# Weight loads of two MLP layers issued by GpSimd instead of SyncE

## The chip, the core and the metric

The kernel runs on one core of one Trainium2 chip. The metric is the device time of one execution in microseconds. SyncE (SP) only issues transfers here; TensorE (PE), VectorE (DVE) and ScalarE (ACT) compute; GpSimd (POOL) does nothing in the kernel before beyond four fills at the start.

## What is computed

```python
# attention on 4 batches x 8 heads x 576 positions x 64, then two dense layers on 2304 tokens
out_d = sm_attn(q_d, k_d, v_d)                 # q, k, v averaged over 4 neighbours
out_up = np.repeat(out_d, factor, axis=2)
mask = np.abs(pos[:, None] - pos[None, :]) < factor          # a band of 7 keys
out_local = softmax(where(mask, scale * q @ k.T, -1e9)) @ v
x = (out_up + out_local) as [2304, 512]
h = x @ w_in                                   # 512 -> 2048
x = (maximum(h, 0) + alpha * minimum(h, 0)) @ w_out          # 2048 -> 512
h = x @ w_in2
out = where(h > 0, h, exp(minimum(h, 0)) - 1) @ w_out2
```

The weights arrive as 64-bit floats, so one tile of 128 by 512 is 512 KB.

## The kernel before

Each of the two layers has 32 weight tiles, i0, o0, i1, o1 and so on to i15, o15 (`items`): tile i of a pair feeds the matmuls x @ w_in, tile o those of @ w_out, for one slice of 128 hidden units. A tile is loaded raw (`load_w`, L314: name rawi or rawo) and then converted (`th_conv`, L1192): ACT copies the high half (cp), DVE shifts and merges it in three instructions (cp, cw, cw), ACT rounds the result (wi or wo) and DVE forms the remainder (wi or wo). Matmuls with a tile need all of it. PE runs the attention of the batches between the matmuls of the layers.

A Python scheduler writes the order of every engine's instructions when the kernel is built. It keeps a clock per engine (`_Clock`) with assumed costs, transfers included (`dma`, L166), and steps small generators ("threads") by priority. So a change in the assumed cost of a transfer moves instructions on all engines. All transfers stand in one queue, issued by SP in the written order; an SP instruction that waits for a semaphore holds all behind it.

The first batch uses buffers of later weight tiles: q and k lie in those of i12 to o15, v in those of i8 to o9 (`load_v0`), the operands of the dense local attention, vd and dP, in those of i6 to o7 and i4 to o5. `th_ldw` (L1226) lets a tile's load start only when its buffer is free: for i4 to o5 and i6 to o7 that is after the matmuls dP,vd of one of the four head pairs (`pav`). From the fifth tile on it also waits until the tile four places earlier is converted (`cv`, PF = 4).

The band of the first batch's second half goes through DRAM to be laid out as rows of 7: ACT copies scores to ss (two buffers), SP writes them to scr, SP reads the diagonal as s, DVE and ACT form the softmax a, SP writes a into pscr (a DRAM area filled with zeros by two transfers beforehand), SP reads it as pp, PE transposes pp (`th_S0`, `th_soft0`, `th_p`). ACT and DVE take their instructions in order, so an ss, s or ppT that is late holds the conversions behind it. xsp is a spill of x, mask a constant.

Of the kernel before, what the change touches and what calls it, by code (L numbers as in the profile page):

```python
# [7 lines left out]
F32 = mybir.dt.float32  # L8
# [9 lines left out]
NP = H // 2  # L18
# [24 lines left out]
PB, FB, RB, PF, CS = 1000.0, 300.0, 300.0, 4, 6  # L43
# [14 lines left out]
class _Clock:  # L58
# [2 lines left out]
           ("DVE", "DVE"): 127.0, ("DVE", "PE"): 179.0, ("DVE", "SP"): 120.0, ("PE", "ACT"): 197.0,  # L61
           ("PE", "DVE"): 196.0, ("PE", "SP"): 189.0, ("DMA", "SP"): 900.0, ("DMA", "ACT"): 907.0,
           ("DMA", "DVE"): 907.0, ("DMA", "PE"): 1003.0, ("ACT", "ACT"): 140.0}
    MANY = {"ACT": 70.0, "DVE": 93.0, "SP": 50.0, "PE": 0.0}

    def __init__(self):
        self.cols = {}
        self.t = dict.fromkeys(("PE", "ACT", "DVE", "SP", "DMA"), 0.0)
        self.t["SP"] = 560.0
        self.hw = 0.0  # L70
        self.seen = {}
        self.share = 1.0
        self.uses, self.bar, self.slots, self.count = {}, {}, {}, {}
        self.cur = self.ctx()
# [41 lines left out]
    def deps(self, eng, outs, ins):  # L116
# [13 lines left out]
        for src, e in last.items():  # L130
            if e > self.seen.get((eng, src), 0.0):
                self.seen[eng, src] = e
                n += 1
                t = max(t, e + self.LAG.get((src, eng), 0.0))
        return t + (self.MANY[eng] if n > 1 else 0.0)

# [26 lines left out]
            n, want = n * k, want * k  # L163
        return n * (8 if ap.dtype == U64 else 4)

    def dma(self, out, in_):  # L166
        outs, ins = [self.span(out)], [self.span(in_)]
        n = int(out.shape[0]) * _free(out) * (8 if out.dtype == U64 else 4)
        piece = min(self.run(out), self.run(in_))
        cost = max(n / 360 * (2 if piece < 512 else 1), n / piece / 16 * 7)  # L170
        self.t["SP"] = max(self.t["SP"], self.deps("SP", outs, ins))
        self.hw = max(self.hw + 25, self.t["SP"]) + 450
        end = max(self.t["DMA"], self.hw + 650) + cost
        self.t["DMA"] = end
        self.note("DMA", outs, ins, end)
        c = self.cur
        c["t"] = max(c["t"], end + 900)
        c["on"] = "DMA"


def _free(ap):
    n = 1
    for d in ap.shape[1:]:
        n *= int(d)
    return n


class _Engine:
# [31 lines left out]
    def __getattr__(self, op):  # L220
        fn = getattr(self.eng, op)

        def call(*args, **kw):
            if op == "dma_start":
                self.clock.dma(kw["out"], kw["in_"])
            else:
                outs = [kw[k] for k in ("out", "accum_out") if k in kw] + list(args[:1])
                ins = [a for k, a in kw.items() if k not in ("out", "accum_out") and hasattr(a, "ap")]
                wait = 0.6 * int(kw["lhsT"].shape[1]) if op == "matmul" else 0.0
                self.clock.op(self.name, *self.cost(op, kw, args), outs, ins + list(args[1:]), wait)  # L230
            return fn(*args, **kw)  # L231
        return call
# [3 lines left out]
def fused_kernel(ctx: ExitStack, tc: tile.TileContext, qk, vt, vl, ql, kl, vb, w_in1, w_out1, alpha,  # L236
                 w_in2, w_out2, ident_d, mask_d, zero_d, vd, maskd_d, out):
    nc = tc.nc
    ck = _Clock()
    PE, ACT, DVE, SP = (_Engine(n, e, ck) for n, e in  # L240
                        (("PE", nc.tensor), ("ACT", nc.scalar), ("DVE", nc.vector), ("SP", nc.sync)))

    const = ctx.enter_context(tc.tile_pool(name="const", bufs=1))
    wp = ctx.enter_context(tc.tile_pool(name="w", bufs=1))
# [10 lines left out]
    maskb = const.tile([128, 5, QK], BF16, name="maskb")  # L255
    identb = const.tile([128, 128], BF16, name="identb")
    warm = const.tile([128, 4], BF16, name="warm")

    W = {}
    raw = {}  # L260
# [51 lines left out]
    wsrc = {(1, "i"): w_in1, (1, "o"): w_out1, (2, "i"): w_in2, (2, "o"): w_out2}  # L312

    def load_w(key):  # L314
        ly, nm, f = key
        if wide:
            raw[key] = wp.tile([128, 512], U64, tag=f"w{nm}{f}", name=f"raw{nm}{f}")
            SP.dma_start(out=raw[key], in_=wsrc[ly, nm][f])

    gs = {}  # L320
    cp = {}
# [19 lines left out]
    st = {}  # L341
# [408 lines left out]
    def finish(*key):  # L750
        done[key] = ck.cur["t"]
# [474 lines left out]
    def th_ldw(ly):  # L1226
        for k, it in enumerate(items):
            if ly == 2:
                yield "key", "fr", (2,) + it
            else:  # L1230
                if PT0 <= k < PP0:
                    yield "key", "pav", 0, k - PT0, 0
                elif PP0 <= k < V0:
                    yield "key", "pav", 0, k - PP0, 0
                elif V0 <= k < SH0:
                    yield "key", "sv", 0, k - V0
                elif k >= QK0:
                    yield "key", "dav", (k - QK0) // 2, (1,)
                    for u in range(2):
                        yield "key", "smm", 0, (k - QK0) // 2, u  # L1240
                if k >= PF:
                    yield "key", "cv", 1, k - PF
            yield ("DMA",)
            load_w((ly,) + it)
            finish("ld", (ly,) + it)
            ck.cur["t"] = now[0]
# [185 lines left out]
    with tc.manual_schedule():  # L1432
# [32 lines left out]
        spawn(th_soft0(0, 1), -10, 0)  # L1465
        spawn(th_vb(0, 1), UV, 0)
        spawn(th_ldw(1), 0)
        for k in range(2 * NF):
            spawn(th_conv(1, k), k / CS, early=ECONV)
# [29 lines left out]
        for s in range(NS1 + NS2):  # L1499
            slot[0] = s if s else -1  # L1500
            ly, g, f, first, last, i = seq[s]
# [3 lines left out]
            if s == T7:  # L1505
                assert all(t["p"] < -50 for t in threads), [t["w"] for t in threads]
                pA.__exit__(None, None, None)
                pC = tc.tile_pool(name="pC", bufs=1)
                cp["pool"] = pC.__enter__()
                tokens.update({"x2": [0.0], "x2s": [0.0, 0.0], "cp": [0.0] * 2, "cw": [0.0] * 2, "os": [0.0] * 4})  # L1510
                spawn(th_ldw(2), 0)
                for k in range(2 * NF):
                    spawn(th_conv(2, k), 2 + k / 100)
                for gg in range(NG2):
                    spawn(th_x2(gg), gg)
# [5 lines left out]
            key = (ly, "i", f)  # L1521
# [124 lines left out]
```

## Time and profile before

| what | value |
|---|---|
| device time, median of 3 runs | 969.86 us (968.71 to 970.83) |
| device time of the profiled execution | 970.52 us |
| its span | 968.7 us |
| PE busy | 938.5 us, 97% of the span |
| DVE busy | 599.5 us, 62% |
| ACT busy | 471.3 us, 49% |
| transfers moved | 86.17 MB, mean 89 GB/s |

The span runs from the first to the last instruction that the profile shows; 1.8 us of the device time lie around it. All sums below start from the profiled execution. PE is busy in nearly all of the span, but before about 110 us it also runs short matmuls of no use (tile warm), runs part of the time at half clock, and waits.

### The profile page before, as it was taken

How to read it: one execution, taken by the hardware profiler on the slowest of the kernel's cores; microseconds unless marked ns; L12 is line 12 of the kernel's file. 1: busy time of each engine (PE TensorE's matmuls, PEld its weight loads, DVE VectorE, ACT ScalarE, POOL GpSimd, SP SyncE). 2: the span in 40 equal slices, each digit the busy share in tenths (PEclk: the TensorE clock that was granted, in tenths of full speed). 3: DMA queues.
4: the chain of work that ended last, by engine and by line, in shares of the span. 5: the costliest groups of instructions: out<-in, count | busy, mean ns of one | idle time of the engine just before them, and what ended most of it. 6: DMA issues, size and time to landing. Idle time of an engine off the chain costs nothing.

```text
span 968.7 us, 16336 instructions
## 1 busy us (share of the span) xinstructions
PE 938.5 (97%) x6428; PEld 866.0 (89%) x6428; DVE 599.5 (62%) x1253; ACT 471.3 (49%) x1200; POOL 0.2 (0%) x4
## 2 busy tenths in 40 slices
PE   5978999899999999999999999999999999999998
PEld 3767889799999899999999999989999999998997
DVE  5778998645959789899638999732322322322222
ACT  5575678555432572332326677644443433433433
POOL 0000000000000000000000000000000000000000
PEclk9687999989999999999999999999999999999999
DMA  9277762534111523100207950003100100000000
GB/s 291 93 247 228 240 222 52 102 110 160 50 31 54 167 70 90 33 19 37 82 1 238 377 195 33 1 1 98 55 12 1 66 1 1 33 1 1 33 1 32
DMA packets 60933, 86.17 MB, mean 89 GB/s; under 512 B 29279, under 2 KB 40415, under 8 KB 60599
## 3 DMA queue, kind: packets, MB, share of 16 engines
q1 hardware_dynamic: 60857, 85.14, 28.0%
q8 instruction: 50, 0.82, 0.4%
q14 instruction: 26, 0.21, 0.1%
HBM read 69.93 MB, written 16.63 MB: 89 GB/s over the span
## 4 chain that ended last, share of the span: by engine, by line
PE 89%; DMA 6%; ACT 2%; DVE 2%; issue 1%; SPq 1%; ACTq 0%
PE bank L231 89%; DMA scr<-ss 2%; DMA s<-scr 1%; DMA qk<-in_qk_dram 1%; DMA pp<-pscr 1%; DMA pscr<-a 1%; SPq L231 1%; ACT dP L231 0%; DVE cw L231 0%; ACT ss L231 0%; ACT cp L231 0%; ACT P L231 0%; DVE s L231 0%; ACT n L231 0%; DVE cp L231 0%
## 5 line engine op out<-in xcount | busy, mean ns | idle before, releaser
L231 PE MATMUL bank<-xh,wi 128*128 128x288 f32 x1024 | 240.6, 304 | 3.6 <-DVE wi L231 2.8
L231 ACT ACTIVATE n<-bank 128x288 f32<-128x288 f32 (+1 forms) x224 | 99.4, 444 | 290.7 <-PE bank L231 290.5
L231 PE MATMUL bank<-gh,wo 128*128 128x288 f32 x1024 | 237.1, 302 | 1.2 <-ACT ys L231 1.2
L231 PE MATMUL bank<-x2h,wi 128*128 128x384 f32 x768 | 211.2, 337 | 0.0
L231 PEld LDWEIGHTS bank<-xh,wi 128*128 128x128 f32 x1024 | 176.4, 191 | 8.6 <-DVE wi L231 3.9
L231 PEld LDWEIGHTS bank<-gh,wo 128*128 128x128 f32 x1024 | 174.4, 190 | 6.3 <-issue 2.9
L231 PE MATMUL bank<-wo,gh 128*128 128x512 f32 x576 | 179.0, 392 | 0.0
L231 DVE SCALAR_TENSOR_TENSOR r<-n,bank 128x384 f32<-128x384 f32 x96 | 53.1, 554 | 195.0 <-ACT n L231 194.9
L231 ACT ACTIVATE gh<-r 128x288 fp32r<-128x288 f32 (+1 forms) x224 | 106.8, 477 | 100.2 <-DVE r L231 99.7
L231 PE MATMUL bank<-xl,wi 128*128 128x288 f32 x512 | 152.9, 299 | 0.0
L231 PE MATMUL bank<-gl,wo 128*128 128x288 f32 x512 | 151.8, 297 | 0.0
L231 DVE TENSOR_TENSOR gl<-r,gh 128x288 fp32r<-128x288 f32 (+1 forms) x224 | 111.4, 498 | 60.8 <-ACT gh L231 59.2
L231 PEld LDWEIGHTS bank<-x2h,wi 128*128 128x128 f32 x768 | 140.3, 188 | 3.9
L231 PE MATMUL bank<-x2l,wi 128*128 128x384 f32 x384 | 128.9, 336 | 0.0
L231 PEld LDWEIGHTS bank<-wo,gh 128*128 128x128 f32 x576 | 106.8, 188 | 18.2
L231 PE MATMUL bank<-wo,gl 128*128 128x512 f32 x288 | 113.8, 395 | 0.0
L231 DVE SCALAR_TENSOR_TENSOR r<-n,nal,bank 128x288 f32<-128x288 f32 x128 | 65.2, 509 | 53.1 <-ACT n L231 52.5
L231 PEld LDWEIGHTS bank<-xl,wi 128*128 128x128 f32 x512 | 98.0, 191 | 0.0
L231 PEld LDWEIGHTS bank<-gl,wo 128*128 128x128 f32 x512 | 97.3, 190 | 0.0
L231 PEld LDWEIGHTS bank<-x2l,wi 128*128 128x128 f32 x384 | 72.1, 188 | 3.8
L231 PEld LDWEIGHTS bank<-wo,gl 128*128 128x128 f32 x288 | 54.0, 187 | 11.5
L231 ACT ACTIVATE n<-n 128x384 f32<-128x384 f32 x96 | 50.4, 525 | 3.1
(101 smaller groups left out, 895.6 us busy)
## 6 DMA issues: line engine op xcount, KB each, us to landing
rawi<-in_w_in_dram SPq DMA_DIRECT2D x32, 512.0 KB
rawo<-in_w_out_dram SPq DMA_DIRECT2D x32, 512.0 KB
qk<-in_qk_dram SPq DMA_DIRECT2D x12, 582.0 KB
yT<-ys SPq DMA_DIRECT2D x32, 144.0 KB
out_dram<-os SPq DMA_DIRECT2D x18, 256.0 KB
vl<-in_vl_dram SPq DMA_DIRECT2D x4, 960.0 KB
vv<-in_vt_dram SPq DMA_DIRECT2D x12, 288.0 KB
kls<-in_kl_dram SPq DMA_DIRECT2D x12, 288.0 KB
```

Source lines behind the costliest of these rows:

```text
L231: return fn(*args, **kw)
```

## The change

The loads of raw weight tiles are issued by GpSimd, on its own queue. GpSimd's first instruction is a copy of one column of the last v tile of the first batch into a new tile, pace; it waits until that v has landed, and all weight loads stand behind it. The wait of a load for the conversion four tiles earlier is gone; the waits for free buffers stay. The scheduler's clock gets an engine GP, whose transfers cost that engine 1000 units each.

```diff
-    def dma(self, out, in_):
+    def dma(self, out, in_, eng="SP"):
...
-        self.t["SP"] = max(self.t["SP"], self.deps("SP", outs, ins))
-        self.hw = max(self.hw + 25, self.t["SP"]) + 450
-        end = max(self.t["DMA"], self.hw + 650) + cost
+        self.t[eng] = max(self.t[eng], self.deps(eng, outs, ins))
+        if eng == "SP":
+            self.hw = max(self.hw + 25, self.t["SP"]) + 450
+            end = max(self.t["DMA"], self.hw + 650) + cost
+        else:
+            self.t[eng] += 1000
+            end = max(self.t["DMA"], self.t[eng] + 650) + cost
...
+    pace = const.tile([128, 1], F32, name="pace")
...
-            SP.dma_start(out=raw[key], in_=wsrc[ly, nm][f])
+            GP.dma_start(out=raw[key], in_=wsrc[ly, nm][f])
...
-                if k >= PF:
-                    yield "key", "cv", 1, k - PF
+                if not k:
+                    yield "key", "ldv", NP - 1
+                    nc.gpsimd.tensor_copy(out=pace, in_=st["vv", 0, NP - 1][:, 0:1])
```

The order of instructions shows what moves. First SP, from the second write of scores to the read s of the first batch; before:

```order
L231 DMA scr0_1_94<-ss_584 72x624 [waits DMAHW5_49,Activation_49]
L231 DMA rawo2_592<-in_w_out1_dram 128x512 [waits DMAHW6_49]
L231 DMA rawi3_623<-in_w_in1_dram 128x512 [waits DMAHW7_49]
L231 DMA rawo3_653<-in_w_out1_dram 128x512 [waits DMAHW0_49]
L231 DMA scr0_1_94<-ss_646 72x624 [waits DMAHW1_49,Activation_49]
L231 DMA vb_675<-in_vb_dram 78x2048 [waits DMAHW2_49]
L231 DMA rawi4_692<-in_w_in1_dram 128x512 [waits DMAHW3_49,PE_49]
L231 DMA scr0_1_94<-ss_671 72x624 [waits DMAHW4_49,Activation_49]
L231 DMA qk_724<-in_qk_dram 128x1164 [waits DMAHW5_49]
L231 DMA vv_726<-in_vt_dram 128x576 [waits DMAHW6_49]
L231 DMA rawo4_758<-in_w_out1_dram 128x512 [waits DMAHW7_49,PE_49]
L231 DMA s0_777<-scr0_1_94 72x32x7 [waits DMAHW4_49,DMAHW1_49,DMAHW0_49]
```

The same engine with the change, from the spill xsp on to the first pp:

```order
L235 DMA xsp_91<-x_375 128x1152 [waits DMAHW3_49,DVE_49]
L235 DMA mask_75<-in_mask_dram 128x182 [waits DMAHW4_49]
L235 DMA pscr1_99<-in_zero_dram 12x14982 [waits DMAHW5_49]
L235 DMA pscr0_98<-in_zero_dram 12x14982 [waits DMAHW6_49]
L235 DMA scr0_1_95<-ss_568 72x624 [waits DMAHW7_49,Activation_49]
L235 DMA scr0_1_95<-ss_600 72x624 [waits DMAHW0_49,Activation_49]
L235 DMA scr0_1_95<-ss_678 72x624 [waits DMAHW1_49,Activation_49]
L235 DMA scr0_1_95<-ss_716 72x624 [waits DMAHW2_49,Activation_49]
L235 DMA s0_762<-scr0_1_95 72x32x7 [waits DMAHW3_49,DMAHW2_49,DMAHW7_49,DMAHW1_49,DMAHW0_49]
L235 DMA pscr1_99<-a_845 72x32x7 [waits DMAHW5_49,DMAHW4_49,DVE_49]
L235 DMA pp_923<-pscr1_99 72x624 [waits DMAHW4_49]
L235 DMA pp_925<-pscr1_99 72x624 [waits DMAHW6_49]
```

All weight loads are gone from SP; vb, qk and vv, which stood between the writes of scr, come later, behind pp. GpSimd, which issued nothing, now begins like this (semaphores DMAHW belong to SP's transfers, DMASW to GpSimd's; pace and the first five loads):

```order
L1249 COPY pace_81<-v0_3_138 128x1 [waits DMAHW0_49]
L235 DMA rawi0_273<-in_w_in1_dram 128x512
L235 DMA rawo0_275<-in_w_out1_dram 128x512
L235 DMA rawi1_277<-in_w_in1_dram 128x512
L235 DMA rawo1_290<-in_w_out1_dram 128x512
L235 DMA rawi2_305<-in_w_in1_dram 128x512
```

and from the load of i5 on, whose buffer is that of the third dP, it goes on like this:

```order
L235 DMA rawi5_486<-in_w_in1_dram 128x512 [waits DVE_49,DMASW2_49,PE_49,Activation_49]
L235 DMA rawo5_535<-in_w_out1_dram 128x512 [waits DVE_49,DMASW3_49,PE_49,Activation_49]
L235 DMA rawi6_637<-in_w_in1_dram 128x512 [waits DMAHW1_49,DMASW4_49]
L235 DMA rawo6_654<-in_w_out1_dram 128x512 [waits DMAHW5_49,DMASW5_49]
L235 DMA rawi7_675<-in_w_in1_dram 128x512 [waits DMAHW1_49,DMASW6_49]
L235 DMA rawo7_686<-in_w_out1_dram 128x512 [waits DMAHW2_49,DMASW7_49]
L235 DMA rawi8_695<-in_w_in1_dram 128x512 [waits DMASW0_49]
L235 DMA rawo8_720<-in_w_out1_dram 128x512 [waits DMASW1_49,DVE_49]
L235 DMA rawi9_748<-in_w_in1_dram 128x512 [waits DMAHW4_49,DMASW2_49,DVE_49]
L235 DMA rawo9_788<-in_w_out1_dram 128x512 [waits DMASW3_49,DVE_49,Pool_49]
```

Up to o3 the loads wait for nothing but pace and GpSimd itself; i4 to o5 wait for PE, and i6 to o11 stand behind o5 with only waits for transfers and for work on v that is older, and each for the load eight places earlier.

Second, ACT around the third and fourth copy of scores (ss_646 and ss_671); before:

```order
L231 ACTIVATE P_603,dsum_627<-P_603,dmx_606 72x144 x2
L231 ACTIVATE n_630<-bank5_71 128x288
L231 ACTIVATE ss_646<-bank7_73 72x312
L231 ACTIVATE ss_646<-bank6_72 72x312
L231 ACTIVATE gh_636<-r_631 128x288
L231 ACTIVATE P_603<-P_603,dsum_627 72x144 x2
L231 ACTIVATE P_620,dsum_659<-P_620,dmx_650 72x144 x2
L231 ACTIVATE ss_671<-bank7_73 72x312
L231 ACTIVATE ss_671<-bank6_72 72x312
```

With the change (ss_678 and ss_716), from n on:

```order
L235 ACTIVATE n_644<-bank5_71 128x288
L235 ACTIVATE cp_649<-rawo2_326 128x512
L235 ACTIVATE P_617<-P_617,dsum_641 72x144 x2
L235 ACTIVATE gh_652<-r_645 128x288
L235 ACTIVATE P_634,dsum_663<-P_634,dmx_658 72x144 x2
L235 ACTIVATE ss_678<-bank7_73 72x312
L235 ACTIVATE ss_678<-bank6_72 72x312
L235 ACTIVATE wi2_683<-cw_627 128x512
L235 ACTIVATE P_634<-P_634,dsum_663 72x144 x2
L235 ACTIVATE cp_700<-rawi3_344 128x512
L235 ACTIVATE ss_716<-bank7_73 72x312
L235 ACTIVATE ss_716<-bank6_72 72x312
```

The third copy of scores now stands behind one more cp, the two P groups and gh; the fourth behind another wi and cp.

Third, DVE just ahead of the first softmax on s; before:

```order
L231 TENSOR_REDUCE dmx_785<-P_779 72x2
L231 TENSOR_SCALAR dmx_785<-dmx_785 72x2
L231 TENSOR_SCALAR cp_764<-cp_764 128x512
L231 TENSOR_TENSOR gl_776<-r_767,gh_775 128x288
L231 SCALAR_TENSOR_TENSOR wi3_795<-cw_740,wi3_795 128x512
L231 TENSOR_SCALAR dsum_799<-dsum_799 72x2
L231 RECIPROCAL dsum_799<-dsum_799 72x2
L231 SCALAR_TENSOR_TENSOR cw_817<-rawo3_653,cp_764 128x512
L231 SCALAR_TENSOR_TENSOR cw_817<-rawo3_653,cw_817 128x512
L231 SCALAR_TENSOR_TENSOR s2_820<-s0_777,mask_75 72x224
```

With the change:

```order
L235 SCALAR_TENSOR_TENSOR wi3_728<-cw_703,wi3_728 128x512
L235 SCALAR_TENSOR_TENSOR cw_750<-rawo3_363,cp_726 128x512
L235 SCALAR_TENSOR_TENSOR cw_750<-rawo3_363,cw_750 128x512
L235 SCALAR_TENSOR_TENSOR r_754<-n_753,nal_76,bank4_70 128x288
L235 TENSOR_SCALAR cp_735<-cp_735 128x512
L235 SCALAR_TENSOR_TENSOR cw_773<-rawi4_380,cp_735 128x512
L235 TENSOR_TENSOR gl_761<-r_754,gh_760 128x288
L235 SCALAR_TENSOR_TENSOR wo3_790<-cw_750,wo3_790 128x512
L235 SCALAR_TENSOR_TENSOR cw_773<-rawi4_380,cw_773 128x512
L235 SCALAR_TENSOR_TENSOR s2_807<-s0_762,mask_75 72x224
```

The softmax now stands behind the whole conversion of o3 and three steps of i4; a P block (dmx, dsum) that stood ahead of it comes later.

## Rows read from the trace of the kernel before

**Rows 1.** The page: the span, and PE's busy time with its share.

```profile
span 968.7 us, 16336 instructions
PE 938.5 (97%) x6428; PEld 866.0 (89%) x6428; DVE 599.5 (62%) x1253; ACT 471.3 (49%) x1200; POOL 0.2 (0%) x4
```

**Rows 2.** Windows: stretch, length, busy time of five engines, PE clock, DMA share, GB/s.

```profile
16.00:24.00 8.00, 6.37 (x60) 4.18 (x55) 7.54 (x23) 6.82 (x32) 0.00 (x0) 0.84 0.96 336
24.00:40.00 16.00, 16.00 (x148) 11.78 (x147) 11.64 (x30) 8.26 (x30) 0.00 (x0) 0.50 0.01 4
40.00:60.00 20.00, 16.96 (x161) 13.31 (x160) 14.95 (x34) 14.56 (x45) 0.00 (x0) 0.87 0.86 290
60.00:80.00 20.00, 13.55 (x99) 10.51 (x98) 16.75 (x39) 12.54 (x38) 0.00 (x0) 0.81 0.56 153
80.00:109.00 29.00, 28.18 (x260) 25.89 (x260) 24.84 (x48) 19.30 (x42) 0.00 (x0) 0.83 0.84 273
109.00:140.00 31.00, 29.60 (x232) 28.73 (x233) 30.40 (x62) 22.11 (x58) 0.00 (x0) 1.00 0.71 231
...
180.00:200.00 20.00, 15.76 (x135) 14.13 (x132) 8.61 (x21) 9.84 (x33) 0.00 (x0) 0.83 0.68 163
```

**Rows 3.** The chain that ended last, 44 to 80 us: start, length, what.

```profile
44.08 7.22 DMA scr<-ss
...
52.02 0.44 ACT gh L231
52.46 1.41 ACT P L231 x6
...
54.52 7.38 DMA scr<-ss
...
61.97 5.31 DMA s<-scr
...
70.84 6.27 DMA pscr<-a
...
77.13 2.73 DMA pp<-pscr
```

**Rows 4.** SP's queue in order of time: start, length, what it issued.

```profile
9.75 0.33 SPq L231 DMA_DIRECT2D v<-in_vt_dram  x1
...
40.06 0.33 SPq L231 DMA_DIRECT2D xsp<-x  x1
...
40.91 1.71 SPq L231 DMA_DIRECT2D pscr<-in_zero_dram  x2
44.08 2.34 SPq L231 DMA_DIRECT2D scr<-ss  x2
```

**Rows 5.** ACT in order of time; in brackets the idle time before, and its end.

```profile
24.49 0.66 ACT L231 ACTIVATE cp<-rawi 128x512 f32<-128x512 f32 x1
...
51.39 0.74 ACT L231 ACTIVATE ss<-bank 72x312 f32<-72x312 f32 x2 [1.05 <-DMA scr<-ss]
...
66.33 0.66 ACT L231 ACTIVATE cp<-rawo 128x512 f32<-128x512 f32 x1 [0.37 <-DMA rawo<-in_w_out_dram]
```

**Rows 6.** DVE in order of time, two waits.

```profile
67.30 0.39 DVE L231 SCALAR_TENSOR_TENSOR s<-s,mask 72x224 f32<-72x224 f32 x1 [2.28 <-DMA s<-scr]
...
82.08 0.69 DVE L231 SCALAR_TENSOR_TENSOR wi<-cw,wi 128x512 fp32r<-128x512 f32 x1 [1.92 <-ACT wi L231]
```

**Rows 7.** Groups of DVE instructions up to 210 us: count, busy, mean ns.

```profile
L231 DVE TENSOR_SCALAR cp<-cp 128x512 uint32<-128x512 uint32 x32 | 13.4, 418 | 0.0
...
L231 DVE SCALAR_TENSOR_TENSOR cw<-rawi,cp 128x512 uint32<-128x512 uint32 x16 | 11.1, 692 | 0.5
...
L231 DVE SCALAR_TENSOR_TENSOR wi<-cw,wi 128x512 fp32r<-128x512 f32 x16 | 11.0, 687 | 4.8 <-ACT wi L231 4.6
```

**Rows 8.** PE in order of time: the last dP,vd, and its wait for tile i9.

```profile
38.17 1.28 PE L231 MATMUL bank<-dP,vd 70*64 70x64 f32 x20
...
109.25 0.54 PE L231 MATMUL bank<-xh,wi 128*128 128x288 f32 x2 [1.07 <-DVE wi L231]
```

More of the change, by code (lines that the diff above doesn't have):

```diff
@@ L63 @@
            ("DMA", "DVE"): 907.0, ("DMA", "PE"): 1003.0, ("ACT", "ACT"): 140.0}
-    MANY = {"ACT": 70.0, "DVE": 93.0, "SP": 50.0, "PE": 0.0}
+    MANY = {"ACT": 70.0, "DVE": 93.0, "SP": 50.0, "PE": 0.0, "GP": 50.0}
     def __init__(self):
         self.cols = {}
-        self.t = dict.fromkeys(("PE", "ACT", "DVE", "SP", "DMA"), 0.0)
+        self.t = dict.fromkeys(("PE", "ACT", "DVE", "SP", "DMA", "GP"), 0.0)
         self.t["SP"] = 560.0
@@ L224, in call @@
             if op == "dma_start":
-                self.clock.dma(kw["out"], kw["in_"])
+                self.clock.dma(kw["out"], kw["in_"], self.name)
             else:
@@ L239, in fused_kernel @@
     ck = _Clock()
-    PE, ACT, DVE, SP = (_Engine(n, e, ck) for n, e in
-                        (("PE", nc.tensor), ("ACT", nc.scalar), ("DVE", nc.vector), ("SP", nc.sync)))
+    PE, ACT, DVE, SP, GP = (_Engine(n, e, ck) for n, e in
+                            (("PE", nc.tensor), ("ACT", nc.scalar), ("DVE", nc.vector), ("SP", nc.sync),
+                             ("GP", nc.gpsimd)))
     const = ctx.enter_context(tc.tile_pool(name="const", bufs=1))
```

## The prediction

> **What bounds the kernel now.** The page comes first: PE is busy for 938.5 of 968.7 us [rows 1], so only something that lets PE begin its long matmuls sooner or later, or makes it stop, moves the end. The windows tell where that can be. From 109 to 140 us PE is busy for 29.60 of 31 us at full clock; before that its clock is at 0.81 to 0.87 of full, and from 60 to 80 us it works for 13.55 of 20 us only [rows 2]. Up to about 109 us PE is behind the conversion of weight tiles. DVE does the most of it: a tile costs it one cp (418 ns), two cw (692 ns each) and one wi (687 ns) [rows 7], in sum 2.49 us, 5.0 us for a pair. The last tile that PE waits for in this part is i9: PE stands idle 1.07 us for it and starts at 109.25 [rows 8]. From there on I count PE as the bound (it loses 1.4 us of the next 31), so the end moves with what DVE loses before i9. DVE is busy for 14.95 + 16.75 + 24.84 of the 69 us from 40 to 109 [rows 2]; it stands idle for 12.5 us, in pieces. The pieces that the change touches are a wait of 2.28 us for s and one of 1.92 us, at 82.08, for ACT's rounding of a tile (wi) [rows 6]. Behind them stands the path of the band: ACT can't copy a third ss before the first write of scr has read its buffer (1.05 us, at 51.39), and the chain of waits runs over scr (7.22, then 7.38 us), s (5.31), pscr (6.27) and pp (2.73) [rows 3, 5]. The loads themselves are hardly waited for: 0.37 us once, at rawo [rows 5].
>
> So the loads that the change sets free do not hold the kernel up. What can count is what they do to the band's small transfers, and what the new order puts behind these.
>
> **Term A, the start: 0.** In both kernels v and the weight tiles come last ahead of the first conversion. v is issued at 9.75 [rows 4], and from 16 to 24 us the transfers move some 2.7 MB, five tiles and little else [rows 2]; so v has landed at about 16.5, an estimate. The first tile would then start with pace, take the 2.73 us of a plain transfer (the row of pp [rows 3]) plus 1.5 us for 512 KB at the 336 GB/s of that window, and be there at 20.5 to 21. ACT reads it first at 24.49 [rows 5]. The 3.5 us between are the cover; without them each late us would be a us of conversion. I take 0, bounds 0 to +2.
>
> **Term B, ACT held at the third ss: +1.8 us on DVE.** From 24 to 40 us the transfers are idle (0.01 of their time, 4 GB/s [rows 2]): all buffers are full. The last dP,vd ends at 38.17 + 1.28 = 39.45 [rows 8]. Then 13 tiles (o5 to o11, with buffers that the attention gives back or that i0 to i3 leave), 6.7 MB, can run on GpSimd's queue, with nothing between them but their issue. SP's queue starts xsp at 40.06 and the two pscr fills at 40.91 [rows 4]: 576 KB, 91 KB of mask and 2 x 702 KB stand ahead of the first scr of 175.5 KB. Before, that scr landed at 44.08 + 7.22 = 51.30 [rows 3], 11.24 us after xsp was issued. With the 2.73 us that even a free transfer takes, 8.5 us of it are bytes. No weight load stood in that part of SP's queue; now GpSimd's run beside it. If the two queues don't disturb each other, scr lands at 51.3 again; if they share evenly, at 59.8. No row of before has two queues busy with data, so I bound it by these two and take a point nearer to the second, three quarters, since the transfers are then busy for 0.86 of the time with 290 GB/s already [rows 2]: 57.7.
>
> When does ACT ask? The second ss pair was behind it by 50.34, where it began to wait (51.39 - 1.05 [rows 5]). Now the third copy stands behind one more cp (0.66 [rows 5]), gh (0.44) and the P groups (1.41 [rows 3]), so ACT comes at 52.85 and is held for 4.9 instead of 1.05 us. DVE has three steps of 0.69 us [rows 7] ready that need nothing of ACT, 2.1 us. So 4.9 - 1.05 - 2.1 = +1.8. Bounds: -1 (the old wait goes) and +3.8 (59.8).
>
> **Term C, s: +1.5 us.** The fourth scr was issued 3.1 us after the third copy began (51.39 to 54.52 [rows 3, 5]); now 57.7 + 3.1 = 60.8. It had taken 7.38 us behind vb and three tiles on SP's queue; those are gone from it, so between 2.73 us and 7.38, I take 4.0: 64.8. s itself took 5.31; beside 2.6 MB of weights that by then are still to come (9.4 MB in all, at 290 to 320 GB/s since 39.45) I add 2, so 7.3: it lands at 72.1. The ends are 64 (no sharing, and the short price of scr) and 78 (everything doubled).
>
> DVE now comes later to the softmax too. It had asked for s at 67.30 - 2.28 = 65.0. The order puts one more cp and three steps of 0.69 ahead, 2.5 us, less a P block of about 1 us that now stands behind: +1.5. With term B it asks at 68.3, and waits 3.8 where it waited 2.28 [rows 6]: +1.5. Bounds: -2.3 (s there already) and +5.3. Conversions behind s are late by that much, and PE with them, as these are the tiles it waits for up to i9.
>
> **Term D, pscr and pp: -0.9 us.** s lands later, so a, pscr (6.27) and pp (2.73 [rows 3]) follow: 72.1 + 3.5 of softmax + 9.0 = 84.6. In PE's order the first transposition of pp now stands behind 102 instead of 78 matmuls of the layers, so PE asks later as well. vb, qk and vv now stand behind pp on SP and are asked for late in the second batch's work, so I give them nothing. The wait of 1.92 us of DVE for ACT at 82.08 [rows 6] should get about half shorter because ACT is less bound up with ppT: -0.9. Bounds -1.9 and +2.
>
> **Later: 0.** From 180 to 200 us PE stands idle for 4.2 us at a clock of 0.83 [rows 2]. That is the second batch's band; the weights have been loaded by then in both kernels, and the order around it is the same from there on. Bounds -2 and +2.
>
> **Sum.** 0 + 1.8 + 1.5 - 0.9 + 0 = +2.4 us against the profiled execution's 970.5, so 972.9; the median shown is 0.66 lower than that execution, so I forecast **972.3 us**. Its own range, with one of B and C a third off, is 970 to 976.
>
> **A rule beside term B.** The row shows 290 GB/s at a share of 0.86 from one queue [rows 2]: little room for a second one. The Trainium skill, page "DMA: Bandwidth & Descriptors", section "Issuing engines are not separate DMA queues", says that transfers started by different engines run on the same 16 DMA engines and interleave, so a second issuer saves only the sequencer's issuing time. By that rule the loads come no sooner and the band's transfers share fully, which is the second rival below; the trace agrees as far as its one queue goes, and no run here has yet shown two.
>
> **The rivals.**
> *Faster.* SP's queue is short now: scr has no vb and tiles ahead of it. If the two queues hardly disturb each other, the first scr lands before about 54 and s before 65; then ACT's 1.05 and DVE's 2.28 of waiting go and some 1.9 at 82 us [rows 5, 6]. That is -5.2 in sum: 964.6. For it speaks that the scr after 54.52 took 7.38 us [rows 3] behind tiles that no longer stand there; against it the 0.86. It decides by the landing of the first scr. Chance 0.33.
> *Hidden.* DVE's 12.5 us of slack take the later s up, or the terms cancel: 969.9, within 0.2% (about 1.9 us, what a measurement can tell from no change). Chance 0.23.
> *Full sharing.* The bounds of B and C at once, +3.8 and +5.3, less 0.9: +8.2 on the profiled execution, 978.7, or 978.1 beside the median. Chance 0.06.
> *DVE slowed by GpSimd's issuing.* GpSimd now works on 19 tiles while DVE converts. If each holds one cp of DVE for its own length again, 19 x 0.42 [rows 7] = 8.0 us: 977.9. DVE's cp rows would be longer than 418 ns in the median. POOL did nothing beside it before [rows 1], so the rows tell nothing. Chance 0.06. The Trainium skill, page "SBUF — State Buffer", section "Who interferes with whom", says that GpSimd's building of descriptors and DVE's two-port operations lock each other out of a shared port pair; no run here has shown it yet.
> *The first loads too late.* If v lands at 20, the first tile comes at 24.2 plus the issue and ACT waits from 24.49 on. Chance 0.02: about 974.
>
> **How the numbers follow.** The forecast has 0.30. Slower by over 0.2% hold the forecast, full sharing, the slowed DVE and late loads: 0.44. Faster 0.33, the same 0.23. The range of 8 in 10 reaches from the faster rival, 964, to 979 past full sharing; beyond the two ends I leave some 0.2. Both signs are inside it, so the forecast's own 970 to 976 stands above.
>
> **What would show it.** Term A: ACT's first cp of rawi still at about 24.5 without a wait for a transfer. Term B: the first scr lands at 57 to 58, ACT's wait for it is near 5 us, and the transfers are busy from 39.5 to 65. Term C: DVE's wait for s near 3.8 us, s landing at 72. Term D: the wait at wi after pp near 1 us. The sum: the end of DVE's conversion of i9, and with it PE's start on that tile, at about 111.6 instead of 109.25 [rows 8], and PE without new idle time behind it. I am wrong if scr lands before 54; if DVE's cp gets longer; if PE's idle time at 180 to 200 us changes by more than 2 us, since that would be a term that I set to nothing; or if i9 moves and the end does not move with it.

## The result, and the profile after

The changed kernel takes 976.95 us (median of 6 runs, 975.12 to 980.81), the kernel before 969.13 us (6 runs, 967.52 to 970.83). The ratio is 1.0085, 95% interval 1.0061 to 1.0109: slower by 0.6 to 1.1%. The forecast was 972.3 us: the sign was right, the loss about three times what was forecast (+7.8 us between the medians and +8.2 between the profiled executions, 978.75 and 970.52 us, instead of +2.4). The median lies outside the forecast's own range, 970 to 976, and inside the wider one of 8 in 10, 964 to 979.

The page of the changed kernel, its first lines and its first two transfer queues (packets, MB, share of the 16 engines); q0 is the queue of GpSimd:

```profile
span 977.0 us, 16335 instructions
...
PE 933.0 (96%) x6407; PEld 862.0 (88%) x6407; DVE 599.4 (61%) x1253; ACT 470.5 (48%) x1200; POOL 35.0 (4%) x69
...
q1 hardware_dynamic: 51641, 51.58, 18.3%
q0 software_dynamic: 9216, 33.56, 9.4%
```

DVE is busy for as long as before, PE for 5.5 us less [rows 1]. The windows of the changed kernel, columns as in [rows 2]:

```profile
24.00:40.00 16.00, 16.00 (x145) 11.84 (x142) 11.26 (x30) 8.22 (x29) 2.05 (x4) 0.50 0.62 225
40.00:60.00 20.00, 13.56 (x114) 10.56 (x113) 15.91 (x35) 13.53 (x39) 6.25 (x12) 0.67 0.97 354
60.00:80.00 20.00, 9.61 (x71) 7.79 (x69) 8.82 (x20) 6.94 (x21) 2.65 (x5) 0.76 0.69 239
80.00:109.00 29.00, 24.33 (x190) 21.94 (x189) 25.35 (x52) 17.30 (x47) 2.12 (x4) 0.80 0.63 184
109.00:140.00 31.00, 29.74 (x269) 27.92 (x269) 27.84 (x54) 20.65 (x49) 0.00 (x0) 0.94 0.31 86
180.00:200.00 20.00, 19.11 (x197) 17.51 (x196) 12.17 (x31) 12.93 (x41) 0.00 (x0) 1.00 0.61 110
200.00:240.00 40.00, 38.16 (x396) 34.76 (x395) 18.78 (x44) 24.38 (x79) 0.00 (x0) 1.00 0.42 111
500.00:600.00 100.00, 97.49 (x661) 94.59 (x661) 82.89 (x163) 61.36 (x131) 17.31 (x32) 1.00 0.56 197
```

The hole is from 60 to 80 us: DVE works for 8.82 us where it worked for 16.75, PE for 9.61 instead of 13.55, while the transfers move 239 instead of 153 GB/s [rows 2]. The chain of waits of the changed kernel names what is in the hole:

```profile
43.50 10.50 DMA scr<-ss
...
58.03 0.73 ACT ss L235 x2
...
58.78 5.60 DMA scr<-ss
...
64.51 11.82 DMA s<-scr
...
95.57 9.04 DMA vb<-in_vb_dram
```

s took 11.82 us instead of 5.31, the first scr 10.50 instead of 7.22 [rows 3]. DVE, PE and ACT of the changed kernel in order of time, with the idle time before in brackets:

```profile
76.36 0.39 DVE L235 SCALAR_TENSOR_TENSOR s<-s,mask 72x224 f32<-72x224 f32 x1 [10.84 <-DMA s<-scr]
...
116.21 0.69 DVE L235 SCALAR_TENSOR_TENSOR wi<-cw,wi 128x512 fp32r<-128x512 f32 x1
```

```profile
55.40 0.61 PE L235 MATMUL bank<-xh,wi 128*128 128x288 f32 x1 [6.42 <-ACT wi L235]
...
78.65 0.75 PE L235 MATMUL bank<-qk 64*72 64x144 f32 x2 [10.39 <-ACT od L235]
```

```profile
23.87 0.67 ACT L235 ACTIVATE cp<-rawi 128x512 f32<-128x512 f32 x1
...
54.08 0.74 ACT L235 ACTIVATE ss<-bank 72x312 f32<-72x312 f32 x2 [2.02 <-DMA scr<-ss]
```

DVE waits 10.84 us for s where it waited 2.28 [rows 6], and with it ACT and PE. s landed some 9 us later than before: 2.5 us because it was issued later, 6.5 because it took longer. The second DVE row is tile i9, done at 116.90. Before, it was done at 109.20 and PE started on it at 109.25 [rows 8], so i9 is 7.7 us late. Of the rest, PE loses 2.5 us between 500 and 600 us (before2, below: 0.06) and gains 1.5 between 180 and 240 (idle for 0.89 + 1.84 instead of 4.24 us; before, 200 to 240 had no idle time). 7.7 + 2.5 - 1.5 = 8.7 against the 8.3 us by which the span grew.

What runs beside s: the queues of the changed kernel from the issue of s to its end (packets, MB, share of the 16 engines' time).

```profile
q0 software_dynamic: 811, 2.92, 67.4%
q1 hardware_dynamic: 2316, 0.06, 11.4%
```

All 2,304 pieces of s, 63 KB, share the engines with 2.92 MB of weights.

### The profile page after: what moved, and what is told of

It is laid out like the page before. It is cut to its first block, busy times and chain, and to the rows that moved or that the text cites. A ratio compares the mean times of both kernels' runs of the same rounds, so it can differ in the third digit from the quotient of the medians.

```text
span 977.0 us, 16335 instructions
## 1 busy us (share of the span) xinstructions
PE 933.0 (96%) x6407; PEld 862.0 (88%) x6407; DVE 599.4 (61%) x1253; ACT 470.5 (48%) x1200; POOL 35.0 (4%) x69
## 4 chain that ended last, share of the span: by engine, by line
PE 88%; DMA 7%; ACT 3%; DVE 2%; issue 1%; SPq 0%; ACTq 0%; DVEq 0%
PE bank L235 88%; DMA scr<-ss 2%; DMA yT<-ys 2%; DMA s<-scr 1%; DMA vb<-in_vb_dram 1%; ACT dP L235 1%; DMA ident<-in_ident_dram 0%; ACT ys L235 0%; DMA pp<-pscr 0%; DVE dmx L235 0%; ACT ss L235 0%; ACT P L235 0%; DVE Dmx L235 0%; ACT n L235 0%; SPq L235 0%
## 5 line engine op out<-in xcount | busy, mean ns | idle before, releaser
L235 DVE SCALAR_TENSOR_TENSOR r<-n,nal,bank 128x288 f32<-128x288 f32 x128 | 65.3, 510 | 58.2 <-ACT n L235 57.7
```

## The experiments

Theory S: the loads of the second queue take the transfer engines from the band's small transfers. Theory O: the new written order costs the time. Two edits keep the order before and change the queue alone; the others keep the changed order of PE, ACT and DVE row for row (in t1s and mix up to the second pair of layers) and change only which loads go, and when. Ratios are to the kernel before on the same chip.

| run | order of PE, ACT, DVE | weight loads | ratio (95%) |
|---|---|---|---|
| light | changed | o5 to o13 left out | 0.9992 (0.9971 to 1.0013) |
| hold12 | changed | from i6 behind s | 1.0148 (1.0110 to 1.0186) |
| pp12 | changed | from i6 behind the first pp | 1.0101 (1.0066 to 1.0137) |
| pp16 | changed | from i8 behind the first pp | 1.0073 (1.0047 to 1.0098) |
| queue | before | free | 1.0255 (1.0212 to 1.0297) |
| qhold | before | from o4 behind s | 1.0249 (1.0200 to 1.0298) |
| small | changed | 2 x 256 KB a tile | 1.0090 (1.0056 to 1.0123) |
| t4 | changed | four under way | 1.0164 (1.0115 to 1.0213) |
| t1 | changed | one under way | 1.0154 (1.0122 to 1.0186) |
| t1s | changed | one; second pair on SyncE | 1.0127 (1.0097 to 1.0157) |
| mix | changed | one, then two; second pair on SyncE | 1.0018 (0.9994 to 1.0042) |

**light.** The loads of 17 tiles are left out, and their conversions read a finished tile instead.

```diff
+    def real(key):
+        t = W[1, "i", 0].rearrange("p a n -> p (a n)").bitcast(U64) if key in skip else raw[key]
...
-            GP.dma_start(out=raw[key], in_=wsrc[ly, nm][f])
+            k = 2 * f + (nm == "o")
+            if ly == 1 and 11 <= k < 28:
+                ck.dma(raw[key], wsrc[ly, nm][f], "GP")
+                skip.add(key)
+            else:
+                GP.dma_start(out=raw[key], in_=wsrc[ly, nm][f])
```

> The changed kernel with the same written order; the 17 loads of o5 to o13 are left out, and the conversions of these tiles read the finished tile i0 instead, so part of the weights is not what the reference has. S: with the bytes gone, s takes about 5.3 us, VectorE's wait for s is under 4 us, and the time is 966 to 970 us. O: above 974 us.

963.16 us beside 964.65 us of before on that chip. SyncE issues s at 59.24, and DVE's first operation on it has no wait ahead of it:

```profile
63.56 0.38 DVE L236 SCALAR_TENSOR_TENSOR s<-s,mask 72x224 f32<-72x224 f32 x1
```

With the order of the changed kernel row for row and the bytes of 17 tiles gone, the loss is gone. That speaks for S; O in its plain form falls. The conversions even lead: i9 was done at 102.0 us and o15 at 160.4, before at 109.2 and 166.5. Yet the time is not measurably shorter than before. The trace shows where a large part of the lead goes: light leaves the loads of the second pair on GpSimd, and from 500 to 600 us PE stands idle for 4.18 us (before 0.06), behind ACT, which waits there for writes of yT:

```profile
500.00:600.00 100.00, 95.82 (x607) 91.63 (x607) 88.50 (x171) 65.46 (x136) 17.14 (x32) 0.98 0.59 204
```

So light is no upper bound on what a second queue can give.

**queue.** The old order of PE, ACT and DVE; only the loads go to GpSimd, behind the same copy of v.

```diff
-            SP.dma_start(out=raw[key], in_=wsrc[ly, nm][f])
+            GP.dma_start(out=raw[key], in_=wsrc[ly, nm][f])
```

> The queue alone: the written order of TensorE, VectorE and ScalarE of the kernel before, row for row; the weight loads are issued by GpSimd behind the copy of v, and SyncE keeps the rest in its old order. S: the loads run beside scr and s here too, s takes 8 us or more, VectorE waits 4 to 10 us for it, and the time is 972 to 979 us. O: the old order gives the old time, 967 to 971 us.

989.43 us, worse than S had it (972 to 979), so S missed the size. DVE in order of time:

```profile
81.52 0.39 DVE L231 SCALAR_TENSOR_TENSOR s<-s,mask 72x224 f32<-72x224 f32 x1 [12.60 <-DMA s<-scr]
```

The queue alone costs 2.5% in the old order, more than the queue and the new order together (1.0085). O falls a second time: if anything the new order, which puts more conversions ahead of s, is a help.

**hold12.** GpSimd stops ahead of i6 until s has landed.

```diff
+        if held:
+            nc.gpsimd.tensor_copy(out=pace[0:BLK], in_=st["s", b, u][:, 0, 0, 0:1])
+            for o, w in held:
+                nc.gpsimd.dma_start(out=o, in_=w)
```

> The changed kernel, with the written order of TensorE, VectorE, ScalarE and SyncE kept to the row; only GpSimd holds the loads from i6 on until s of the first batch has landed (it copies one column of s). Theory S (the weight loads of the second queue take the transfer engines from the band's small transfers): s takes 5 to 6 us instead of 11.8, VectorE's wait for s falls from 10.8 to under 4 us, ScalarE's wait at the third ss goes, and the time comes to 967 to 971 us. Theory O (the new written order itself costs the time, whatever the transfers do): s is shorter, but the kernel stays above 974 us.

978.59 us: a miss. s behaved as S said (issued at 56.13, DVE started on it at 60.45 without a wait), but the time did not come back. PE of hold12, and the queues while a is written into pscr (64.5 to 88 us):

```profile
90.84 1.15 PE L235 MATMUL bank<-ident,pp 72*78 72x72 f32 x8 [15.98 <-DMA pp<-pscr]
```

```profile
q0 software_dynamic: 2293, 8.34, 88.9%
q1 hardware_dynamic: 2316, 0.06, 5.5%
```

The held loads were let go one behind the other from 59.9 us on, just as the next small transfer of the band started, and 8.34 MB of weights moved beside it. SyncE issued the write into pscr at 64.55 and could issue the first pp only at 88.11. The loss moved from s to pscr.

The same view shows how the transfer engines were shared here. Two stretches of 2 us: 76.5 to 78.5, while weights kept coming, and 84.5 to 86.5, when they ran out.

```profile
q0 software_dynamic: 220, 0.82, 99.9%
q1 hardware_dynamic: 162, 0.00, 4.6%
...
q0 software_dynamic: 142, 0.50, 61.4%
q1 hardware_dynamic: 750, 0.02, 21.1%
```

Beside the stream 162 small packets went for 220 of the weights, which are some 3.7 KB each, and so it was in every 2 us from 68.5 to 84.5 (144 to 170 for 219 to 230). So some three packets of SyncE's queue went for four of GpSimd's, whatever their size: by bytes it is 4.5 KB (162 times 28 bytes) for 0.82 MB. At some 80 packets per us the 2,304 pieces of such a transfer need 28 us, an estimate from these counts.

**qhold.** The same hold in the order of queue.

> As the run named queue, with the loads from o4 on held until s of the first batch has landed. S: scr and s have the transfer engines to themselves, and stand behind no tile on SyncE's queue, so s lands some 2 to 4 us earlier than before and VectorE's wait of 2.28 us goes: 965 to 969 us. O: no different from queue.

988.99 us, the same miss. Its chain of waits:

```profile
56.57 3.74 DMA s<-scr
...
68.22 27.39 DMA pscr<-a
```

s took 3.74 us with the engines to itself, and the write into pscr, which carries as many pieces as s, 27.39 us beside the flood, near the 28 us estimated from hold12; before it took 6.27 [rows 3].

**pp12 and pp16.** The hold reaches to the first pp; in pp16 four more tiles go ahead of it.

```diff
+        if (b, p, u) == (0, 0, 1):
+            nc.gpsimd.tensor_copy(out=pace[0:BLK], in_=st["pp", b, p, u][:, 0, 0, 0:1])
+            for o, w in held:
+                nc.gpsimd.dma_start(out=o, in_=w)
```

> As hold12 (same written order on the four other engines), but GpSimd holds the loads from i6 on until the first pp has landed, not only s. S: no weight load runs beside scr, s or the write into pscr; s takes 5 to 6 us, the write into pscr about 5 instead of 23, o5 is converted near 76 to 80 us instead of 93.7, ScalarE waits at most 3 us for i6, and the kernel is at 0.997 to 1.001 of the kernel before. Were hold12's loss not the flood's move onto the write into pscr, pp12 would stay at 1.01.

> As pp12, but four more tiles (i6 to o7, 2 MB) are let go at 39 to 44 us, beside xsp, the fills of pscr and the first scr. S: the first scr lands 2 to 5 us later than in pp12, s and pscr are undisturbed; 0.998 to 1.004 of the kernel before.

973.84 and 971.21 us, beside 963.63 us of before: two misses. s and pscr were free (pscr 5.34 us in pp12), but the flood met what comes next on SyncE's queue. The chain of waits and PE of pp12:

```profile
67.71 5.34 DMA pscr<-a
...
87.85 11.66 DMA vb<-in_vb_dram
```

```profile
99.55 2.19 PE L235 MATMUL bank<-ppT,vb 78*64 78x72 f32 x32 [4.27 <-DMA vb<-in_vb_dram]
```

Wherever it was let go, the flood held up the transfer that then stood at the front of SyncE's queue: s, pscr or vb.

**small.** Each load in two transfers, with pieces of 1 KB in the program.

```diff
-            GP.dma_start(out=raw[key], in_=wsrc[ly, nm][f])
+            for b in range(2):
+                o, w = (t.rearrange("p (a b n) -> p a b n", a=2, b=2)[:, :, b] for t in (raw[key], wsrc[ly, nm][f]))
+                nc.gpsimd.dma_start(out=o, in_=w)
```

> The changed kernel with the same written order; each weight load is made in two transfers of 256 KB whose pieces are 1 KB instead of 4 KB, same bytes. If the transfer engines take turns by piece, s (2,304 pieces of 28 bytes) ends well before the weight loads that run beside it do, takes 6 to 9 us instead of 11.8, and the kernel gains 3 us or more on the changed one (ratio near 1.004). If they share by bytes, or serve the older queue first, s again ends when the weight loads end, and the ratio stays near 1.0085 or rises because of twice the issues.

974.25 us, ratio 1.009. s in the chain of waits, and the weights beside it:

```profile
63.22 5.43 DMA s<-scr
```

```profile
q0 software_dynamic: 257, 0.85, 54.7%
```

s took 5.43 us, but this run doesn't settle how the engines take turns: 257 packets for 0.85 MB of weights are 3.3 KB each, so the packets had hardly become smaller, and with twice the issues the engines moved 172 GB/s beside s, in the changed kernel 255. What small shows is that s is hardly harmed beside a thinner stream, and that s is not all: the time did not come back, against 1.004 expected with turns by piece. i9 was done at 109.6 us, as early as before, but o15 at 172.7 instead of 166.5, and ACT waited 3.34 us, at 127 us, for a write of yT0a. Whether that is all of the loss isn't shown.

**t1, t4.** GpSimd copies one column of an earlier tile (one place back in t1, below, and four in t4) ahead of each load from o4 on, so that one or four loads are under way.

```diff
+            if ly == 1 and k >= 9:
+                last = (1,) + items[k - 1]
+                t = raw[last] if last in raw else W.get(last)
...
+                    nc.gpsimd.tensor_copy(out=pace, in_=t.bitcast(F32)[:, 1:2])
...
             GP.dma_start(out=raw[key], in_=wsrc[ly, nm][f])
```

> The changed kernel with the same written order; from o4 on GpSimd issues a load only when the load before it has landed (it copies one column of that tile), so one load is under way at a time instead of up to eight. S, in the form that a small transfer shares the engines with as many weight pieces as are queued: s takes 5 to 8 us, the write into pscr under 8, vb under 7; at about 4 us a tile the loads still lead the conversions; i9 is converted at 102 to 106 us and the kernel is at 0.996 to 1.003 of the kernel before. If the number under way doesn't matter, s stays near 12 us and the ratio near 1.0085.

> As t1, but four loads under way (GpSimd waits for the load four places earlier). S: between the two: s 7 to 11 us, 1.002 to 1.008 of the kernel before.

s in the chain of waits of t1, and of t4:

```profile
57.26 4.89 DMA s<-scr
```

```profile
66.71 12.92 DMA s<-scr
```

One load under way leaves s alone; four are as bad as eight (11.82). The weights that moved beside s tell why: 0.52 MB in t1, through by about 60 us, after which 906 small packets went in half a us; 3.72 MB in t4, more than the 2.92 of the changed kernel. t4 takes 980.92 us, a miss. In t1 all tiles up to i9 are early (i9 at 100.3 us, before 109.2, expected 102 to 106; 2.6 us of the lead are there at i0 already, with a granted clock of 0.68 instead of 0.50 from 24 to 40 us). Yet t1 takes 978.32 us, a miss for another reason. Its ACT, 97 to 104 us:

```profile
97.45 0.68 ACT L235 ACTIVATE cp<-rawo 128x512 f32<-128x512 f32 x1 [3.47 <-DMA rawo<-in_w_out_dram]
...
103.77 0.66 ACT L235 ACTIVATE cp<-rawi 128x512 f32<-128x512 f32 x1 [4.48 <-DMA rawi<-in_w_in_dram]
```

One at a time, a tile comes every 5 us or so (issues at 93.46, 98.12, 104.79, 110.00), slower than the conversions take them; from o9 on the loads, which nothing had waited for, are the bound.

**t1s.** As t1, with the second pair's loads on SyncE again.

```diff
-            GP.dma_start(out=raw[key], in_=wsrc[ly, nm][f])
+            (GP if ly == 1 else SP).dma_start(out=raw[key], in_=wsrc[ly, nm][f])
```

> As t1 for the first pair of layers, with the 32 loads of the second pair issued by SyncE as before. S: t1 without TensorE's idle time of 2 to 3 us between 500 and 600 us, where the loads of the second pair run beside the writes of yT: 0.993 to 1.000 of the kernel before. If that idle time has another cause, no different from t1.

976.71 us, again above what was expected. The window 500 to 600 us of t1, then of t1s:

```profile
500.00:600.00 100.00, 97.21 (x648) 93.93 (x648) 85.52 (x169) 63.89 (x136) 17.53 (x32) 1.00 0.59 204
```

```profile
500.00:600.00 100.00, 99.94 (x673) 97.09 (x671) 85.95 (x169) 63.73 (x136) 0.00 (x0) 1.00 0.58 205
```

PE's idle time there goes from 2.8 to 0.1 us at the same GB/s. So the second place of loss is shown too: the second pair's loads, from GpSimd, hold up other transfers; in the changed kernel ACT waits 1.86 us there, at 578 us, for a write of yT. The medians of t1 and t1s differ by 1.6 us, within what the two intervals allow.

**mix.** As t1s, from o8 on with two loads under way.

```diff
-                last = (1,) + items[k - 1]
+                last = (1,) + items[k - (1 if k < 17 else 2)]
```

> As t1s up to i8: one load under way from o4 on, the second pair's loads on SyncE; from o8 on two loads under way, since t1 and t1s kept the changed order's lead up to i9 (100.3 us against 109.2 before) and then lost it where o9 to i12 came in late, at about 5 us a tile. Theory: two under way bring a tile every 2.5 to 3 us, conversions and scr of the second batch are not held; o15 is converted at 158 to 163 us and the kernel is at 0.993 to 1.000 of the kernel before. Rival: two under way hold up scr and the writes of yT of the second batch as eight did the first batch's; 1.003 to 1.010.

968.08 us (12 runs) beside 965.56 us (17 runs): the best version that computes everything, and not to be told from the kernel before. The profile is of one of its slowest executions (972.07 us). PE in order of time:

```profile
94.88 1.22 PE L235 MATMUL bank<-ppT,vb 78*64 78x72 f32 x32 [1.52 <-DMA vb<-in_vb_dram]
...
125.98 0.51 PE L235 MATMUL bank<-gh,wo 128*128 128x288 f32 x1 [3.36 <-ACT ys L235]
```

With two under way the waits are back in small: 1.52 us for vb, and 3.36 us where ACT waited for a write of yT0a (6.46 us in the chain). o15 was converted at 170.8 us, not at 158 to 163. The theory's part on the loads held in the main: a load was issued every 3.4 us or so from o8 on, instead of 2.5 to 3, and no conversion waited for one. The rival's waits took part of the gain; how much of it isn't shown.

**before2.** The kernel before, profiled again.

> The kernel before again, one look, for its profile beside those of the other runs: the same waits (s 2 to 3 us, the third ss 1 us), and a time between 959 and 972 us, by the clock that TensorE is granted ahead of 110 us.

965.19 us. Its windows 24 to 40 and 500 to 600 us:

```profile
24.00:40.00 16.00, 13.61 (x177) 9.69 (x171) 14.21 (x35) 10.10 (x36) 0.00 (x0) 1.00 0.27 93
500.00:600.00 100.00, 99.94 (x649) 96.22 (x649) 92.13 (x180) 67.78 (x143) 0.00 (x0) 1.00 0.58 204
```

The waits are those of before, the one for s shorter than expected (1.13 us). From 500 to 600 us PE has no idle time. From 24 to 40 us the granted clock is 1.00, where the first profile had 0.50 [rows 2]; i0 is done at 34.9 instead of 37.5 us. So two executions of one program can differ by this much ahead of the first tile.

## Why the prediction was right in sign and short in size

**The bound.** Right. The end moved with the conversions: i9 by 7.7 us, the last tile, o15, from 166.5 to 175.4, the span by 8.3.

**Term A, 0.** Right. v had landed by 16.3 us; ACT's first cp came at 23.87 without a wait, before at 24.49 [rows 5].

**Term B.** ACT's wait grew as forecast, but by less: the first scr landed at 54.0 (forecast 57.7), and ACT waited 2.02 us (forecast 4.9). The wait did reach PE, 6.42 us at 55.40, but DVE hardly: it asked for s at 65.5, 0.5 us later than before, where the order was to bring 1.5 and this term 1.8 more. Three quarters of full alternation was too much for scr.

**Term C is the step that failed**: "beside 2.6 MB of weights that by then are still to come ... I add 2, so 7.3". s was issued at 64.51 (forecast 64.8) and took 11.82 us, above even the 10.6 that doubling gives, with 2.92 MB beside it. The price was wrong. I had charged s its share of bytes, as if 63 KB beside 2.6 MB were a question of bandwidth. The runs show that a transfer of 2,304 small pieces is held much longer: s 11.82 and 12.92, pscr 27.39 us beside a flood, 4.9 us beside one load, 3.74 alone. Where weights kept coming, hold12 moved about 80 pieces per us; in the changed kernel 956 of the 2,316 small packets went only from 73.5 us on, when the weights ran out. DVE asked for s at 65.5 (forecast 68.3) and waited 10.84 us (forecast 3.8), so the term is +8.6 instead of +1.5. Of the 7.0 us that its wait is longer than forecast, 4.5 are the length of s and 2.8 that DVE came earlier than forecast, less 0.3 for the earlier issue of s.

The amount of weights came near by luck: of the 9.4 MB, 290 to 320 GB/s from 39.45 to 64.8 leave 1.3 to 2.1 MB, not 2.6, and the 13 tiles that were counted leave out i12 to o13, which GpSimd issued from 62.21 to 67.38. Nor do 970 to 976 follow from "one of B and C a third off", which is some 0.6 us.

**Term D.** Not as forecast. DVE's longest wait for ACT behind pp was 1.47 us (at 92.62, for a wo; forecast 1, before 1.92), and PE waited 1.65 us for vb, issued at 95.57 behind pp. The prediction gave vb nothing, because it was asked for late; pp12 and pp16 lost 4.3 and 4.0 us by it.

**Later, 0.** From 180 to 200 us PE's idle time fell by 3.35 us, more than the 2 us that the prediction named as a sign of being wrong; 1.84 came back by 240, so the gain of 1.5 was within the term's bounds. Part of the fall is spread: before2, the same program as before, has 2.55 us there instead of 4.24. The 2.5 us at 500 to 600 us were not thought of: the prediction counted the loads of the first pair only, and the change moves 32 more.

**The rivals.** The slowed DVE (977.9) and full sharing (978.1) came nearest in time, but neither by its mechanism: for full sharing scr was to land at 59.8. The faster rival was to be decided by scr landing before 54 us, and by s before 65; scr did come at 54.0, s at 76.3. That DVE is slowed by GpSimd's issuing has fallen: its cp is as long as before [rows 7], in the groups of the changed kernel up to 210 us:

```profile
L235 DVE TENSOR_SCALAR cp<-cp 128x512 uint32<-128x512 uint32 x32 | 13.4, 418 | 0.0
```

So the lock between GpSimd's descriptor building and DVE's two-port operations, of which the Trainium skill tells (page "SBUF — State Buffer", section "Who interferes with whom"), costs DVE nothing that this trace shows. The rule that a second issuer adds no second set of engines (the Trainium skill, page "DMA: Bandwidth & Descriptors", section "Issuing engines are not separate DMA queues") agrees with the runs: loads of GpSimd's queue held transfers of SyncE's, and light, with the bytes gone, has no wait for s.

Open stays where small lost its time, why the turns went by packet, and what a second queue can give with the second pair's loads on SyncE and nothing in the way of the band.

## What to carry to other kernels

A queue that is written in order also paces: here SyncE's order kept 6.7 MB of loads that nobody waited for out of the way of 63 KB that everybody waited for. Before loads are moved to a queue of their own, list what small transfers of the critical path run in that time, and limit how many loads are under way; a hold that lets them all go at once only picks the next victim. Price a small transfer beside a stream by its pieces, not by its bytes. And test for an upper bound early, with all that the change moves left out: light kept the loads of the second pair, and the 4.18 us that PE lost beside them hid what the rest could give.

## What was not expected of the hardware

- The write of 63 KB into pscr, 5 to 6 us otherwise, took 27.39 us beside a flood of weight loads: in hold12 162 packets of 28 bytes went for 220 of 3.7 KB in 2 us.
- One 512 KB load after the other, each waiting for the one before, came at 5 to 5.5 us a tile (some 100 GB/s); with up to eight under way all transfers together moved 354 GB/s (40 to 60 us).
- The granted clock from 24 to 40 us was 0.50 (1.2 GHz) in some profiles and 1.00 (2.4 GHz) in others of the same program: the kernel before had 0.50 in one and 1.00 in the other, with PE busy for 6.37 and 5.71 of the 8 us ahead. Between these two i0 moved by 2.6 us, and the kernel before ranged from 959.5 to 971.45 us on one chip; differences under 0.3% can't be read from single runs of this kernel.
